# wo of one head as two 64-row halves on partitions 0 to 63, by two 32-row loads in eight shares

## The chip, the cores and the metric

The kernel runs on one core of a Trainium2 chip. The metric is the device time of one execution in microseconds. Before the change three runs took 711.59, 712.06 and 712.72 us; the median, 712.06 us, is what the change is compared with.

## The reference

Two layers, applied twice with the same weights, to a batch of four rows of 640 numbers (one token each, decoding from a cache). All is float32.

```python
x = x + _A_ref(_layernorm(x), k_cache, v_cache, wq, wo)   # round one
x = x + _B_ref(_layernorm(x), w1, w2)
x = x + _A_ref(_layernorm(x), k_cache, v_cache, wq, wo)   # round two
x = x + _B_ref(_layernorm(x), w1, w2)

# _A_ref: 32 heads of 128, the last W = 1024 positions of the cache
q = (x @ wq).reshape(B, 1, 32, 128).transpose(0, 2, 1, 3)
scores = einsum("bhqd,bhkd->bhqk", q, k[:, :, -W:]) * 128 ** -0.5
o = einsum("bhqk,bhkd->bhqd", softmax(scores), v[:, :, -W:])
return o.reshape(B, 1, 4096) @ wo                          # wo: 4096 x 640

# _B_ref: relu(x @ w1) @ w2, with w1 640 x 1728 and w2 1728 x 640
```

The head that the change touches is the 26th (number 25 counted from 0) in round one: its part of the last product is `o[:, 25] @ wo[25 * 128 : 26 * 128]`, 128 rows of 640.

## The kernel before

**Data.** The caches and weights of a head lie in HBM as one record of REC = 9472 columns on 128 partitions (the tensor `rec`): 640 columns of wq, 4096 of k, 4096 of v, 640 of wo, in this order (`WQ`, `K`, `V`, `WO` are the columns at which they begin). 32 records are 155 MB. They are read in round one and again in round two but for what is left in SBUF of the last heads. The tensor `wm` holds w1 and w2.

**Places in SBUF.** `store` has room for five records and a part of a sixth; `home(h, r)` says at which column a head's record goes. `kept` holds a part of head 26, `ring` (4320 columns) the MLP's weights in the time between the rounds; its first 128 columns hold an identity at the start, and until the MLP's first load nothing else is in it.

**Loads.** All large loads stand in one list, `items`, in a fixed order, and are issued by SyncE (SP). `pump()` issues from the head of the list for as long as the next load's place is free (`live` is the list of taken places); `done()` is called behind the matmuls that read a piece last, gives its columns back and calls `pump()`. So the order of loads is that of the list, and when one starts is decided by who reads the place last. Most loads are runs of several heads (`GROUPS`, 4 to 8 MB); towards a round's end they become smaller. Head 25 of round one is one load of 9472 columns. Each load takes one of eight semaphores in turn, so SP also waits for the load eight places earlier.

At the end of round one (`ending`) the wo of the last six heads (LATE) comes last, behind all k and v. Then come the MLP's weights into `ring` and the free half of a record.

**Compute.** For each head TensorE makes the query (`query`), the scores (`scores`), the products with v (`values`), the transposed output (`output_T`, a matmul that ScalarE copies from PSUM to `oTs`) and the product with wo (`project`: four matmuls of 160 columns, each with all 128 rows, added up in the PSUM tile `acc`). Heads overlap: while head n is at `values`, head n+1 is at `softmax`, head n+2 at `query`. VectorE and ScalarE do the softmax. `InOrder` keeps each engine's instructions in the written order; since it makes the calls, nearly all rows of the profile have its line, L102, and are told apart by their tiles.

Of the kernel before, what the change touches and what calls it, by code (L numbers as in the profile page):

```python
# [81 lines left out]
FIVE = [REC + 6272, 2 * REC - 3072, 2 * REC - 3200]  # L82
LAST_FIVE = [REC + 4736, 2 * REC - 4736, REC, REC]
THREE = [REC + HALF, REC + HALF]
GROUPS = [{h: FIVE for h in range(0, 25, 5)}, {6: THREE, 9: FIVE, 14: FIVE, 19: LAST_FIVE}]


# [19 lines left out]


@with_exitstack
def decode_kernel(ctx: ExitStack, tc: tile.TileContext, xf, rec, wm, out):  # L110
    nc = tc.nc
    pe, dve, act, pool, sp = (InOrder(tc, e) for e in (nc.tensor, nc.vector, nc.scalar, nc.gpsimd, nc.sync))
    sb = ctx.enter_context(tc.tile_pool(name="sb", bufs=1))
# [10 lines left out]
    hT = scratch.rearrange("p (m j) -> p m j", j=32)  # L124
    oTs = sb.tile([P, LATE, B], F32, name="oTs")
    qT = sb.tile([P, B], F32, name="qT")
    of_batch = sb.tile([P, B], F32, name="of_batch")
    of_block = sb.tile([P, 4], F32, name="of_block")
    rows = sb.tile([P, 2 * B], F32, name="rows")
# [58 lines left out]
    buffers = {"store": store, "ring": ring, "kept": kept}  # L188

    def load(src, lo, hi, buf, col, parts):  # L190
        items.append((src[:, lo:hi], buf, col, hi - lo, parts))

    def place(buf, col):
        return ("store", spare + FROM + col) if buf == "spare" else (buf, col)
# [10 lines left out]

    def piece(r, h, lo, hi, buf="store", col=None):
        run(r, h * REC + lo, h * REC + hi, buf, home(h, r) + lo if col is None else col)


    def group(r, h, sizes):  # L210
# [21 lines left out]
    for h in hs[:-3]:  # L232
        if h in GROUPS[0]:
            group(0, h, GROUPS[0][h])
        if h >= 25:
            piece(0, h, 0, KEPT if h == LAST - 1 else WO if h >= H - LATE else REC)
        if h == LAST - 1:
            piece(0, h, KEPT, WO, "kept", 0)
    ending(0, hs, True)
# [38 lines left out]
    def pump():  # L278

        while items:  # L280
            src, buf, col, n, parts = items[0]
            if any(b == buf and x < col + n and col < y for b, x, y in live):
                return
            sp.dma_start(buffers[buf][:, col:col + n], src)
            live.append((buf, col, col + n))
            for key, lo, hi, c in parts:
                at.setdefault(key, []).append((lo, hi, buf, c))
            items.pop(0)
# [1 line left out]
    def pieces(key):  # L290
        return at[key if key in at else (key[0], 0) + key[2:]]

    def cols(key, lo, n):

        for x, y, buf, col in pieces(key):
            if x <= lo and lo + n <= y:
                return buffers[buf][:, col + lo - x:col + lo - x + n]
        raise KeyError((key, lo, n))

    def done(key, lo, hi):  # L300
# [145 lines left out]
        dve.tensor_tensor(o, o, of_block.unsqueeze(2).to_broadcast([P, 4, DH]), op=OP.mult)  # L446
        dve.tensor_reduce(on[last], o.rearrange("p c d -> p d c"), op=OP.add, axis=AX.X)

    def output_T(i, last=False, to=None):
        to = outs[last][:, :B] if to is None else to  # L450
        pe.matmul(to, on[last], pick, start=True, stop=True)
        act.copy(oTs[:, i], to)

    def project(r, h, i, end):
        key = ("rec", r, h)
        for n in range(NB):
            pe.matmul(acc[32 * n:32 * n + B, :FD], oTs[:, i], cols(key, WO + n * FD, FD),
                      start=False, stop=end, skip_group_check=True)
        done(key, WO, REC)
# [41 lines left out]
    for r in range(2):  # L501
        hs = order[r]
        late = LATE if r == 0 else 2
        center(384 * r, 128)
        query(r, hs[0], 0, True)
        if r:
            busy(192, warm)
        scores(r, hs[0], 0, True)
        softmax(0, (r, hs[1], 1))
        if r:  # L510
            unpark(2)
            unpark(3)
        weights(0, ((0, 1), (1, 2)))
        for n, h in enumerate(hs[:-2]):
            i = n - (H - late)
            s = (n + 1) % 2
            scores(r, hs[n + 1], s)
            if r and not n:
                busy()
            softmax(s)  # L520
            end = n == H - 3
            values(r, h)
            if end:
                for _ in range(4):
# [8 lines left out]
            output_T(max(i, 0), to=None if r and not n else t_ps[:, :B])  # L533
# [70 lines left out]
```

## Time and profile before

| what | before |
|---|---|
| device time, median of 3 runs (lowest, highest) | 712.06 us (711.59, 712.72) |
| span of the profiled execution | 710.7 us |
| what lies around the span, by the lowest and the highest run | 0.9 to 2.0 us |
| moved by DMA | 301.97 MB, mean 425 GB/s |
| TensorE / VectorE / ScalarE busy | 71% / 45% / 14% |
| mean granted clock of TensorE | 0.824 |

The span goes from the first to the last instruction of one execution. The profiled execution's own device time is not listed beside the runs, so it is taken to lie among the three. Shares of busy time are averages over the whole span; the two rounds, the MLP between them and the one at the end have different limits and are read one by one in the prediction.

### The profile page before, as it was taken

What the parts mean: (1) busy time and instruction counts of PE and PEld (TensorE: products, weight loads), DVE (VectorE), ACT (ScalarE), POOL (GpSimd) and SP (SyncE); (2) the same over time, 40 slices, a digit from 0 to 9 for tenths busy, and PEclk for the clock granted to TensorE, in tenths of its full rate; (3) what the DMA queues carried; (4) which work ended last, traced back from release to release, by engine and by line L of the source; (5) the groups of instructions that cost most, each with busy time, mean ns of one, the idle gap of its engine ahead of it and who ended that gap; (6) DMA issues with size and microseconds to landing.
All of it is one profiled execution on the core that took longest, in us unless ns stands there. A gap on an engine that the chain in (4) does not pass through costs nothing.

```text
span 710.7 us, 8613 instructions
## 1 busy us (share of the span) xinstructions
PE 502.4 (71%) x3722; PEld 199.5 (28%) x3722; DVE 317.4 (45%) x645; ACT 99.6 (14%) x210; POOL 1.1 (0%) x9
## 2 busy tenths in 40 slices
PE   0675677576677686868788998756577685695985
PEld 0331322231332222333223333322222231332322
DVE  2252344253443353546541866625244253453661
ACT  0210111011010110111130421201010011011120
POOL 0000000000000000000000000000000000000000
PEclk9987787677676778788999999969687677788899
DMA  9999999999999999999999999999999999999996
GB/s 397 436 416 451 422 435 447 417 435 447 420 429 451 427 429 420 425 444 420 426 404 396 411 425 434 447 429 436 442 431 433 434 428 436 430 427 421 430 427 281
DMA packets 12741, 301.97 MB, mean 425 GB/s; under 512 B 1424, under 2 KB 1568, under 8 KB 4640
## 3 DMA queue, kind: packets, MB, share of 16 engines
q1 hardware_dynamic: 12672, 301.42, 98.9%
q8 instruction: 29, 0.48, 0.2%
q14 instruction: 8, 0.07, 0.0%
q10 hardware_dynamic: 32, 0.01, 0.0%
HBM read 301.34 MB, written 0.08 MB: 424 GB/s over the span
## 4 chain that ended last, share of the span: by engine, by line
DMA 68%; PE 25%; DVE 4%; another core or an unknown queue 1%; ACT 1%; issue 1%; SPq 0%; ACTq 0%
DMA store<-rec 60%; PE sc_ps L102 10%; PE o_ps L102 7%; DMA store<-wm 5%; PE acc L102 3%; PE misc L102 3%; DMA ring<-wm 3%; DVE scratch L102 2%; DVE o_ps L102 2%; PE t_ps L102 2%; ACT oTs L102 1%; DVE small L102 0%; ACT sc_ps L102 0%; DVE sc_ps L102 0%
## 5 line engine op out<-in xcount | busy, mean ns | idle before, releaser
L102 PE MATMUL sc_ps<-store,qT 128*4 128x512 f32 x1024 | 193.7, 852 | 37.8 <-DMA store<-rec 36.4
L102 PE MATMUL misc<-xT,store 128*128 128x4 f32 x620 | 92.8, 276 | 100.6 <-DMA store<-rec 100.0
L102 DVE TENSOR_REDUCE small<-sc_ps 128x1 f32<-128x1024 f32 x64 | 78.4, 1224 | 157.9 <-PE sc_ps L102 157.8
L102 PE MATMUL o_ps<-store,scratch 128*16 128x512 f32 x960 | 142.1, 667 | 4.6 <-DVE scratch L102 2.9
L102 PEld LDWEIGHTS misc<-xT,store 128*128 128x128 f32 x620 | 87.4, 221 | 156.2 <-DMA store<-rec 123.1
L102 ACT ACTIVATE sc_ps<-sc_ps,small 128x1024 f32<-128x1024 f32 x64 | 69.8, 1091 | 325.2 <-DVE small L102 325.2
L102 DVE STREAM_TRANSPOSE sc_ps<-sc_ps 128x1024 f32<-128x1024 f32 (+1 forms) x70 | 81.7, 1167 | 0.1
L102 PEld LDWEIGHTS sc_ps<-store,qT 128*4 128x4 f32 x1024 | 32.7, 107 | 121.2 <-issue 66.4
L102 PEld LDWEIGHTS o_ps<-store,scratch 128*16 128x16 f32 x960 | 32.3, 114 | 118.6 <-issue 100.7
L102 DVE TENSOR_TENSOR o_ps<-o_ps,of_block 128x512 f32<-128x512 f32 x62 | 43.4, 699 | 45.9 <-PE o_ps L102 45.8
L102 DVE TENSOR_TENSOR qT<-misc,rows 128x4 f32<-128x4 f32 x61 | 9.5, 156 | 112.7 <-PE misc L102 112.6
L102 PE MATMUL acc<-store,oTs 128*4 128x160 f32 x488 | 34.6, 365 | 17.1 <-ACT oTs L102 17.0
L102 DVE TENSOR_REDUCE scratch<-o_ps 128x128 f32<-128x512 f32 x62 | 42.9, 692 | 2.1
L102 ACT COPY oTs<-t_ps 128x4 f32<-128x4 f32 x59 | 9.6, 162 | 204.5 <-PE t_ps L102 204.5
L102 PE MATMUL t_ps<-rows,scratch 128*128 128x4 f32 x118 | 25.5, 286 | 11.4 <-DVE scratch L102 10.9
L102 PEld LDWEIGHTS t_ps<-rows,scratch 128*128 128x128 f32 x118 | 21.4, 226 | 17.9 <-DVE scratch L102 14.2
L102 DVE TENSOR_TENSOR scratch<-sc_ps,mrt 128x128 f32<-128x128 f32 (+1 forms) x70 | 19.6, 280 | 2.7
L102 PE MATMUL acc<-kept,small 128*1 128x328 f32 (+2 forms) x54 | 17.4, 428 | 0.0
L99 PE MATMUL acc<-scratch,ring 128*128 128x160 f32 x2 | 0.9, 540 | 22.2 <-DMA scratch<-xf 22.2
L102 DVE TENSOR_SCALAR mrt<-of_batch,small 128x4 f32<-128x4 f32 x64 | 14.7, 230 | 2.2
L102 DVE STREAM_TRANSPOSE scratch<-small 128x32 f32<-128x32 f32 x64 | 12.9, 202 | 2.4 <-ACT sc_ps L102 2.4
L102 PEld LDWEIGHTS acc<-store,oTs 128*4 128x4 f32 x488 | 6.9, 84 | 22.9 <-ACT oTs L102 21.9
(84 smaller groups left out, 123.1 us busy)
## 6 DMA issues: line engine op xcount, KB each, us to landing
store<-rec SPq DMA_DIRECT2D x14, 7872.0 KB, 28.9
store<-rec SPq DMA_DIRECT2D x7, 7936.0 KB, 30.9
store<-rec SPq DMA_DIRECT2D x4, 7104.0 KB
store<-rec SPq DMA_DIRECT2D x11, 2368.0 KB, 34.8
store<-rec SPq DMA_DIRECT2D x3, 4736.0 KB, 27.2
store<-rec SPq DMA_DIRECT2D x2, 4416.0 KB, 28.3
store<-rec SPq DMA_DIRECT2D x5, 1024.0 KB, 20.2
store<-rec SPq DMA_DIRECT2D x1, 4160.0 KB, 20.7
```

Source lines behind the costliest of these rows:

```text
L99: r = build(*args, **kwargs)
L102: r = build(*args, **kwargs)
```

## The change

The record of head 25 is loaded without its wo (8832 columns instead of 9472). Its wo comes from a new tensor in HBM, `halves`, by two more loads, into `ring` columns 128 to 1407: rows 0 to 63 of the wo stand in the first 640 of these columns, rows 64 to 127 in the other 640, both on partitions 0 to 63. Each of the two loads fills 32 partitions with rows of 1280 columns (5120 bytes). The source of a load is written as eight groups of four rows, with a fifth row between groups that is not read, so that its outermost dimension has eight steps.

The product with wo is then made in eight matmuls of 64 rows instead of four of 128. The second four need rows 64 to 127 of the transposed output on partitions 0 to 63; ScalarE makes this copy, `upper`, beside the usual one.

```diff
+SPLIT = 25
+HALVES_AT = 128
...
+    upper = sb.tile([64, B], F32, name="upper")
...
+    def halves_of(r):
+        shares = [(halves[q][:, :4], 32 * q, 32) for q in range(2)]
+        items.append((shares, "ring", HALVES_AT, 2 * D, [(("halves", r), 0, 2 * D, HALVES_AT)]))
...
-            piece(0, h, 0, KEPT if h == LAST - 1 else WO if h >= H - LATE else REC)
+            piece(0, h, 0, KEPT if h == LAST - 1 else WO if h >= H - LATE or h == SPLIT else REC)
+            if h == SPLIT:
+                halves_of(0)
...
-            sp.dma_start(buffers[buf][:, col:col + n], src)
+            for src, row, rows in shares:
+                sp.dma_start(buffers[buf][row:row + rows, col:col + n], src)
...
-    def output_T(i, last=False, to=None):
+    def output_T(i, last=False, to=None, split=False):
         pe.matmul(to, on[last], pick, start=True, stop=True)
         act.copy(oTs[:, i], to)
+        if split:
+            act.copy(upper, to[64:])
...
     def project(r, h, i, end):
         key = ("rec", r, h)
+        if (r, h) == (0, SPLIT):
+            key = ("halves", r)
+            for half, o in ((0, oTs[:64, i]), (1, upper)):
+                for n in range(NB):
+                    pe.matmul(acc[32 * n:32 * n + B, :FD], o, cols(key, half * D + n * FD, FD, 64), start=False,
+                              stop=False, skip_group_check=True)
+            done(key, 0, 2 * D)
+            return
...
+    halves = np.zeros((2, 8, 5, 2 * D), k.dtype)
+    halves[:, :, :4] = np.concatenate([rec[SPLIT, :64, WO:], rec[SPLIT, 64:, WO:]], 1).reshape(2, 8, 4, 2 * D)
```

On SP, the queue of loads near the end of round one's large groups; before, the row of 9472 columns is head 25, the two below it are head 26:

```order
L102 DMA store<-rec 128x15744
L102 DMA store<-rec 128x9472
L102 DMA store<-rec 128x6784
L102 DMA kept<-rec 128x2048
L102 DMA store<-rec 128x8832 x2
```

With the change, the same place:

```order
L104 DMA store<-rec 128x15744
L104 DMA store<-rec 128x8832
L104 DMA ring<-halves 32x1x1280 x2
L104 DMA store<-rec 128x6784
L104 DMA kept<-rec 128x2048
L104 DMA store<-rec 128x8832 x2
```

Head 25's load is shorter by 640 columns, and two loads of 32 rows stand between it and head 26; all later loads keep their order and stand two places further back.

On TensorE, the product with wo of head 25 (`acc`) before, behind the query of head 27 (`misc`) and ahead of that head's scores and of head 26's product with v (`o_ps`, half of it from `kept`):

```order
L102 MATMUL misc<-xT,store 128x4 x5
L102 MATMUL t_ps<-rows,scratch 128x4
L102 MATMUL acc<-store,oTs 4x160 x4
L102 MATMUL sc_ps_74<-store,qT 4x512 x8
L102 MATMUL o_ps<-store,scratch 16x512 x4
L102 MATMUL o_ps<-kept,scratch 16x512 x4
```

With the change:

```order
L104 MATMUL misc<-xT,store 128x4 x5
L104 MATMUL t_ps<-rows,scratch 128x4
L104 MATMUL acc<-ring,oTs 4x160 x4
L104 MATMUL acc<-ring,upper 4x160 x4
L104 MATMUL sc_ps_75<-store,qT 4x512 x8
L104 MATMUL o_ps<-store,scratch 16x512 x4
L104 MATMUL o_ps<-kept,scratch 16x512 x4
```

Four matmuls on `oTs` and `store` have become eight, four on `oTs` and four on `upper`, all reading `ring`; nothing else on TensorE has moved. The new tile `upper` takes 32 bytes of each partition ahead of `store`, `kept` and `ring`, which all begin 32 bytes further on.

More of the change, by code (lines that the diff above doesn't have):

```diff
@@ L109, in decode_kernel @@
 @with_exitstack
-def decode_kernel(ctx: ExitStack, tc: tile.TileContext, xf, rec, wm, out):
+def decode_kernel(ctx: ExitStack, tc: tile.TileContext, xf, rec, halves, wm, out):
     nc = tc.nc
@@ L190, in load @@
     def load(src, lo, hi, buf, col, parts):
-        items.append((src[:, lo:hi], buf, col, hi - lo, parts))
+        items.append(([(src[:, lo:hi], 0, P)], buf, col, hi - lo, parts))
     def place(buf, col):
@@ L280, in pump @@
         while items:
-            src, buf, col, n, parts = items[0]
+            shares, buf, col, n, parts = items[0]
             if any(b == buf and x < col + n and col < y for b, x, y in live):
                 return
-            sp.dma_start(buffers[buf][:, col:col + n], src)
+            for src, row, rows in shares:
+                sp.dma_start(buffers[buf][row:row + rows, col:col + n], src)
             live.append((buf, col, col + n))
@@ L291, in pieces, with cols @@
         return at[key if key in at else (key[0], 0) + key[2:]]
-    def cols(key, lo, n):
+    def cols(key, lo, n, rows=P):
         for x, y, buf, col in pieces(key):
             if x <= lo and lo + n <= y:
-                return buffers[buf][:, col + lo - x:col + lo - x + n]
+                return buffers[buf][:rows, col + lo - x:col + lo - x + n]
         raise KeyError((key, lo, n))
@@ L532, in decode_kernel @@
                 busy(320, sc_ps[n % 2])
-            output_T(max(i, 0), to=None if r and not n else t_ps[:, :B])
+            output_T(max(i, 0), to=None if r and not n else t_ps[:, :B], split=(r, h) == (0, SPLIT))
             if r and not n:
@@ L592 @@
         "rec": rec.transpose(1, 0, 2).reshape(P, H * REC),
+        "halves": halves,
         "wm": np.concatenate([block_rows(np.asarray(B_w1)).transpose(1, 0, 2).reshape(P, KB * FF), *tiles], 1),
```

## The prediction, made before the change was run

> **What bounds the kernel.** I read the page first, then the chain of waits, then the busy time by windows.
>
> ```profile
> span 710.7 us, 8613 instructions
> PE 502.4 (71%) x3722; PEld 199.5 (28%) x3722; DVE 317.4 (45%) x645; ACT 99.6 (14%) x210; POOL 1.1 (0%) x9
> DMA  9999999999999999999999999999999999999996
> q1 hardware_dynamic: 12672, 301.42, 98.9%
> q8 instruction: 29, 0.48, 0.2%
> q14 instruction: 8, 0.07, 0.0%
> q10 hardware_dynamic: 32, 0.01, 0.0%
> DMA 68%; PE 25%; DVE 4%; another core or an unknown queue 1%; ACT 1%; issue 1%; SPq 0%; ACTq 0%
> ```
>
> The 16 DMA engines are busy in every slice; the loads' queue q1 alone fills 98.9% of 16 engines' span. No compute engine comes near. So the time is that of moving 301 MB, and what can still differ is how evenly the 16 engines are loaded and whether any of them runs out of work. The windows show both (columns: the window, its length, busy time of PE, PEld, DVE, ACT and POOL, granted clock, DMA share, GB/s):
>
> ```profile
> 300.00:357.00 57.00, 43.78 (x322) 16.95 (x322) 31.41 (x60) 8.90 (x20) 0.00 (x0) 0.88 1.00 429
> 357.00:372.00 15.00, 12.56 (x112) 3.77 (x112) 6.63 (x20) 5.14 (x10) 0.00 (x0) 1.00 1.02 406
> 372.00:400.00 28.00, 23.41 (x239) 9.76 (x240) 11.11 (x30) 5.20 (x9) 0.00 (x0) 1.00 1.00 394
> 400.00:702.00 302.00, 224.19 (x1684) 88.35 (x1685) 147.29 (x294) 43.36 (x95) 0.00 (x0) 0.82 1.00 432
> 702.50:703.00 0.50, 0.48 (x12) 0.10 (x2) 0.00 (x0) 0.00 (x0) 0.00 (x0) 1.00 0.91 379
> 703.00:703.50 0.50, 0.00 (x0) 0.00 (x0) 0.00 (x0) 0.00 (x0) 0.00 (x0) 1.00 0.74 307
> 703.50:704.00 0.50, 0.00 (x0) 0.00 (x0) 0.00 (x0) 0.00 (x0) 0.00 (x0) 1.00 0.64 261
> 704.00:704.50 0.50, 0.00 (x0) 0.00 (x0) 0.00 (x0) 0.00 (x0) 0.00 (x0) 1.00 0.54 220
> 704.50:705.00 0.50, 0.13 (x4) 0.11 (x8) 0.00 (x0) 0.00 (x0) 0.00 (x0) 1.00 0.39 159
> 705.00:705.50 0.50, 0.50 (x20) 0.40 (x16) 0.00 (x0) 0.00 (x0) 0.00 (x0) 1.00 0.42 169
> 705.50:706.00 0.50, 0.50 (x24) 0.39 (x20) 0.00 (x0) 0.00 (x0) 0.00 (x0) 1.00 0.42 140
> 706.00:706.50 0.50, 0.50 (x19) 0.35 (x14) 0.00 (x0) 0.00 (x0) 0.00 (x0) 1.00 0.17 67
> 706.50:707.00 0.50, 0.50 (x20) 0.34 (x10) 0.00 (x0) 0.00 (x0) 0.00 (x0) 1.00 0.04 15
> ```
>
> The last nine rows are the uneven end. The DMA share falls from 0.91 to 0.04 over some 4.5 us: the engines finish the same list of loads one after another, half of them by about 704.3 (0.54 of 16), one alone after 706.5, until about 706.8 (0.04 x 16 x 0.5 us is 0.3 us). The shares add up to 4.27, times 0.5 us 2.1 us: had all 16 ended together, it would have been at about 704.6, some 2.2 us sooner. That is the most that any evening out can bring.
>
> The unevenness has a cause in the first list: q8, 29 instruction packets in 0.48 MB, 16 KB each. Its 0.2% of 16 engines' span (0.15 to 0.25) is 17 to 28 us, 0.6 to 1.0 us a packet, and the engine that serves one falls behind the others by that and a little more. Followed from packet to packet in the trace's records (each engine's next packet starts where its last one ended), every fetch sets one engine back by about 1.4 us, and the fetches go round eight engines in a fixed order, three or four each; the other eight serve none, only some of the eight small q14 packets. So the eight engines that end last are, all but one, those with fetches. The 32 packets of q10 (the four loads of x, four rows each, with their semaphores) fall on the same four engines each time, none of them in the fetches' rotation, though one of the four runs level with another for a while and is placed by its trend alone.
>
> **The moved bytes.** 432 GB/s over 16 engines is 27.0 GB/s for one. Before, an engine carries 8 of the 128 rows of each load: 8 x 2560 bytes of this wo, 20,480 bytes or 0.76 us. All 16 engines lose that. The two new loads have eight shares of four rows of 5120 bytes each: 40,960 bytes or 1.52 us on each of eight engines, and with ten small packets' overhead (a 4-byte packet of q1 lasts 9 ns in the records) some 1.55 us or a little more. So eight engines carry 0.76 us less and eight 0.79 us more. Which eight is what counts. A load in few shares took the same engines four times over (q10), so I expect eight shares on a fixed set that contains these four. If it is the set without fetches, the engine that ends last, at 706.8, ends 0.76 us sooner, at 706.0. Of the loaded ones most end by 704.3 and the latest, as the records go, at 705.2; with 0.79 us more that is 706.0 too, level with the relieved ones. I take **0.7 us less**; the bounds are 0.76 less and 0.79 more.
>
> [...]
>
> [...]
>
> ```profile
> SPq L102 <- PE acc L102: 355.7, 33, 27.0
> SPq L102 <- DMA store<-rec: 114.2, 18, 38.7
> store<-rec SPq DMA_DIRECT2D x14, 7872.0 KB, 28.9
> store<-rec SPq DMA_DIRECT2D x11, 2368.0 KB, 34.8
> ```
>
> SP waits for places (PE acc) and for the load eight places earlier (DMA store<-rec); still a load lands 29 to 35 us after its issue (last number of the last two rows). At the new loads' place the engines thus have some 30 us of work queued, and the eight that carry none go straight on to head 26. Two more issues and a shift of two in the turn of the eight semaphores cost nothing under that cover; if it were gone, they would cost two issues, below 1 us.
>
> **TensorE and ScalarE at head 25.**
>
> ```profile
> 320.40 0.16 ACT L102 COPY oTs<-t_ps 128x4 f32<-128x4 f32 x1 [7.40 <-PE t_ps L102]
> 320.62 0.71 PE L102 MATMUL acc<-store,oTs 128*4 128x160 f32 x8 [0.31 <-ACT oTs L102]
> 321.11 3.38 PE L102 MATMUL sc_ps<-store,qT 128*4 128x512 f32 x16
> 325.42 2.88 SPq L102 DMA_DIRECT2D store<-rec  x3
> 328.00 1.28 PE L102 MATMUL misc<-xT,store 128*128 128x4 f32 x10 [1.79 <-DMA store<-rec]
> ```
>
> The product with wo starts 0.49 us ahead of the scores (320.62 to 321.11), so doubling it adds 0.5 us, at most the 0.71 us of the row; 64 rows instead of 128 may cost less, and I have no row of that, so nothing to 0.71. The copy to `upper` is another 0.16 us and lies beside the first four matmuls. Behind them on TensorE stand head 27's scores and head 26's product with v, and for the latter waits SP with the loads at 325.42: these start up to 0.9 us later, under 30 us of queued work. TensorE itself waits 1.79 us for a load at 328.00, which takes up the rest. Cost: nothing; uncovered, 0.5 to 0.9 us. The MLP's first load into `ring` now also waits for this product, which is over 35 us sooner.
>
> **Between the rounds**, 357 to 400, the rate falls to 406 and 394 GB/s: the mean engine idles 15 x (1 - 406/432) + 28 x (1 - 394/432) = 3.4 us. There a relieved engine's gain could be lost.
>
> ```profile
> 369.66 6.76 DMA ring<-wm
> 378.88 6.69 DMA ring<-wm
> 385.61 1.30 PE acc L102 x30
> ```
>
> These pieces of the chain of waits are loads on whose last engine the MLP waits and whose end lets the next be issued. The whole stage follows the slowest engine; the early ones idle for it. In the records the slowest finds its next load always queued, with 1.4 us or more to spare, so its gain is kept. Of the loaded eight, one is already 3.1 us behind the first here (after a q14 packet), and 0.79 us more makes it last by some 0.2 us: issues come that little later, within the spare time.
>
> **The sum.** Against the profiled execution: span 710.7 - 0.7 = 710.0 us. The same 0.7 us off the median gives 712.06 - 0.7 = 711.4 us.
>
> **Rivals.**
> - *The gain is lost between the rounds.* If the fetching engines do run dry there, the 0.76 us of round one is idled away and the second half begins as before: 712.1 us. For it speak the 394 GB/s, against it the spare time.
> - *The loaded eight include the last one.* Then it carries 0.79 us more: 712.06 + 0.79 = 712.85 us, slower. It decides as soon as one engine with four fetches is among them; only four of the eight are placed by the records.
> - *The shares are not eight.* Spread over all 16, the bytes are as before: 712.1 us.
> - *The new place costs.* All of `store` moves by 32 bytes. If each packet took one 32-byte step more (32 / 27.0 = 1.2 ns), the 12672 / 16 = 792 packets of an engine would cost 0.94 us: 711.4 + 0.9 = 712.3; from two steps on, 713.2 and more, it is slower than a measurement's doubt. No row shows such a cost, none excludes it.
>
> **How the numbers follow.** The forecast gets 0.56, the lost gain 0.16, the loaded last engine 0.12, no eight shares 0.05, the cost of the place 0.06; 0.05 remain for a gain over 1.4 us, where an earlier MLP helps more than counted. 0.2% (1.4 us) is about what a measurement of this kernel can tell from no change, and the three runs before lie 1.1 us apart. The first four cases all lie within it. Their spread by half a microsecond to either side and the last two give faster 0.10, within 0.82, slower 0.08. The range goes from 710.5, the forecast with such a spread and a little, to 712.9, the loaded last engine: below and above it lie about 0.08 and 0.1.
>
> **What will show it.** Right: in windows of 0.5 us at the end the DMA share falls more steeply and reaches 0 about 0.7 us sooner in the span; the two new loads land some 30 us after issue; the product with wo of head 25 shows 16 rows on TensorE and a wait for a load still stands ahead of head 28's query. Wrong: the share's tail as long as before or longer (the wrong engines), a lower rate from 357 to 400 (gain lost), or below 432 GB/s from 400 to 702 (the place costs).

## The result and the profile after

| | before | after |
|---|---|---|
| device time, median (lowest to highest) | 712.42 us (711.59 to 712.72, 5 runs) | 716.4 us (716.07 to 716.79, 5 runs) |
| ratio after to before, 95% interval | | 1.0056 [1.0044, 1.0068] |
| span of the profiled execution | 710.7 us | 714.4 us |

The change makes the kernel about 4 us (0.6%) slower; the forecast was 711.4 us, and the range ended at 712.9. The same lines of the page as before, now with the change (its line L102 is L104 here):

```profile
span 714.4 us, 8633 instructions
PE 502.9 (70%) x3730; PEld 201.7 (28%) x3730; DVE 317.4 (44%) x645; ACT 99.7 (14%) x211; POOL 1.1 (0%) x9
DMA  9999999999999999999999999999999999999996
q1 hardware_dynamic: 12752, 301.42, 98.9%
q8 instruction: 29, 0.48, 0.3%
DMA 67%; PE 24%; DVE 4%; another core or an unknown queue 3%; ACT 1%; issue 1%; SPq 0%; ACTq 0%
```

Nothing has changed in what bounds it. The loads move the same 301.42 MB, in 80 packets more, the queue still fills 98.9% of 16 engines' span, and that span is 3.7 us longer. So the same bytes took longer on engines that were as busy as before. The windows (columns as in the prediction, the last one GB/s) say where. The first row is of before, the others are with the change:

```profile
0.00:300.00 300.00, 194.77 (x1282) 78.45 (x1282) 120.60 (x242) 36.96 (x77) 1.12 (x9) 0.79 1.00 430
0.00:300.00 300.00, 190.47 (x1280) 76.31 (x1280) 120.04 (x240) 36.96 (x77) 1.12 (x9) 0.80 1.00 429
300.00:357.00 57.00, 45.76 (x332) 17.64 (x331) 31.53 (x63) 8.52 (x20) 0.00 (x0) 0.85 1.00 425
357.00:372.00 15.00, 11.26 (x107) 3.43 (x109) 7.19 (x20) 5.68 (x10) 0.00 (x0) 1.00 1.00 395
372.00:400.00 28.00, 22.77 (x231) 8.74 (x231) 9.08 (x28) 3.99 (x7) 0.00 (x0) 1.00 0.99 381
400.00:702.00 302.00, 226.69 (x1672) 92.40 (x1665) 147.85 (x291) 44.58 (x97) 0.00 (x0) 0.79 1.00 430
705.50:706.00 0.50, 0.50 (x22) 0.40 (x16) 0.00 (x0) 0.00 (x0) 0.00 (x0) 1.00 0.91 374
707.00:707.50 0.50, 0.00 (x0) 0.00 (x0) 0.00 (x0) 0.00 (x0) 0.00 (x0) 1.00 0.58 236
709.00:709.50 0.50, 0.50 (x22) 0.39 (x17) 0.00 (x0) 0.00 (x0) 0.00 (x0) 1.00 0.34 133
710.00:710.50 0.50, 0.50 (x20) 0.39 (x16) 0.00 (x0) 0.00 (x0) 0.00 (x0) 1.00 0.05 20
```

From 400 to 702 us, far behind the change and with a DMA share of 1.00 both times, the rate is 430 GB/s and was 432: 0.5% less, on loads that the change does not touch. Between the rounds it falls more (395 and 381 against 406 and 394). At the end the share falls from 0.91 to 0.05 between 705.5 and 710.5 us; before it did so between 702.5 and 707.

A rate that is lower everywhere points at the single packet. The trace's records hold each packet's duration. Here are the medians of three sizes (62,976 bytes are 15,744 columns of one partition), and the time of all q1 packets, summed up and divided by 16 engines:

| kernel | 62,976 B | 18,944 B | 6912 B | all q1 packets / 16 |
|---|---|---|---|---|
| before | 2324 ns | 705 ns | 262 ns | 703.15 us |
| after | 2327 ns | 708 ns | 266 ns | 706.31 us |

Three to four nanoseconds on the median packet of these sizes, and 4.5 on the mean one of all, are 3.16 us for an engine that serves 708 of them one behind the other (12,752 less 1424 of 4 bytes, which still take 9 ns, by 16). The slowdown also begins ahead of the new loads. Load by load, the landing on the first engine to finish is 0.06 to 0.15 us later than before in the first five loads, up to 96 us, and 0.63 us at 282 us, where the new loads are still to come. The moved bytes take 0.7 off behind that. Then it is 0.84 at 369 us, 2.5 at 388 and 3.57 at the last load: some 1.7 us of it arise in 20 us between the rounds, the rest a little at a time.

### The profile page after: what moved, and what is told of

Read it like the earlier page. It is cut to its first block, busy times and chain, and to the rows that moved or that the text cites. A ratio compares the mean times of both kernels' runs of the same rounds, so it can differ in the third digit from the quotient of the medians.

```text
span 714.4 us, 8633 instructions
## 1 busy us (share of the span) xinstructions
PE 502.9 (70%) x3730; PEld 201.7 (28%) x3730; DVE 317.4 (44%) x645; ACT 99.7 (14%) x211; POOL 1.1 (0%) x9
## 3 DMA queue, kind: packets, MB, share of 16 engines
q1 hardware_dynamic: 12752, 301.42, 98.9%
## 4 chain that ended last, share of the span: by engine, by line
DMA 67%; PE 24%; DVE 4%; another core or an unknown queue 3%; ACT 1%; issue 1%; SPq 0%; ACTq 0%
DMA store<-rec 59%; PE sc_ps L104 9%; PE o_ps L104 7%; DMA store<-wm 5%; PE misc L104 3%; DMA ring<-wm 3%; PE acc L104 3%; DVE scratch L104 2%; PE t_ps L104 2%; DVE o_ps L104 1%; ACT oTs L104 1%; DVE small L104 0%; ACT sc_ps L104 0%; DVE sc_ps L104 0%
## 5 line engine op out<-in xcount | busy, mean ns | idle before, releaser
L104 PE MATMUL sc_ps<-store,qT 128*4 128x512 f32 x1024 | 188.9, 831 | 40.8 <-DMA store<-rec 39.4
L104 PE MATMUL misc<-xT,store 128*128 128x4 f32 x620 | 95.2, 280 | 100.0 <-DMA store<-rec 99.3
L104 DVE TENSOR_REDUCE small<-sc_ps 128x1 f32<-128x1024 f32 x64 | 78.4, 1224 | 156.6 <-PE sc_ps L104 156.4
L104 PE MATMUL o_ps<-store,scratch 128*16 128x512 f32 x960 | 144.2, 677 | 4.3 <-DVE scratch L104 3.0
L104 PEld LDWEIGHTS misc<-xT,store 128*128 128x128 f32 x620 | 89.8, 226 | 157.0 <-DMA store<-rec 122.3
L104 ACT ACTIVATE sc_ps<-sc_ps,small 128x1024 f32<-128x1024 f32 x64 | 69.8, 1091 | 323.4 <-DVE small L104 323.4
L104 DVE STREAM_TRANSPOSE sc_ps<-sc_ps 128x1024 f32<-128x1024 f32 (+1 forms) x70 | 81.7, 1167 | 0.1
L104 PEld LDWEIGHTS sc_ps<-store,qT 128*4 128x4 f32 x1024 | 31.9, 104 | 122.1 <-issue 64.9
L104 PEld LDWEIGHTS o_ps<-store,scratch 128*16 128x16 f32 x960 | 32.2, 113 | 115.8 <-issue 99.3
L104 DVE TENSOR_TENSOR o_ps<-o_ps,of_block 128x512 f32<-128x512 f32 x62 | 43.4, 699 | 48.1 <-PE o_ps L104 48.0
L104 DVE TENSOR_TENSOR qT<-misc,rows 128x4 f32<-128x4 f32 x61 | 9.5, 156 | 114.6 <-PE misc L104 114.6
L104 PE MATMUL acc<-store,oTs 128*4 128x160 f32 x480 | 33.1, 356 | 18.2 <-ACT oTs L104 16.7
L104 DVE TENSOR_REDUCE scratch<-o_ps 128x128 f32<-128x512 f32 x62 | 42.9, 691 | 2.1
L104 ACT COPY oTs<-t_ps 128x4 f32<-128x4 f32 x59 | 9.6, 162 | 208.8 <-PE t_ps L104 208.8
L104 PE MATMUL t_ps<-rows,scratch 128*128 128x4 f32 x118 | 25.5, 287 | 11.8 <-DVE scratch L104 11.1
L104 PEld LDWEIGHTS t_ps<-rows,scratch 128*128 128x128 f32 x118 | 21.5, 227 | 18.1 <-DVE scratch L104 14.8
L104 DVE TENSOR_TENSOR scratch<-sc_ps,mrt 128x128 f32<-128x128 f32 (+1 forms) x70 | 19.6, 280 | 2.7
L104 PE MATMUL acc<-kept,small 128*1 128x328 f32 (+2 forms) x54 | 17.4, 428 | 0.0
L104 DVE TENSOR_SCALAR mrt<-of_batch,small 128x4 f32<-128x4 f32 x64 | 14.7, 229 | 2.2
L104 DVE STREAM_TRANSPOSE scratch<-small 128x32 f32<-128x32 f32 x64 | 12.9, 202 | 2.4 <-ACT sc_ps L104 2.4
L104 PEld LDWEIGHTS acc<-store,oTs 128*4 128x4 f32 x480 | 6.7, 84 | 24.1 <-ACT oTs L104 21.5
## 6 DMA issues: line engine op xcount, KB each, us to landing
store<-rec SPq DMA_DIRECT2D x14, 7872.0 KB, 29.5
```

The costliest lines, as they stand in the source:

```text
L104: r = build(*args, **kwargs)
```

## The experiments

The change does two things that could lengthen packets or unbalance engines: `upper` is allocated ahead of `store`, `kept` and `ring` and shifts them by 32 bytes (`store` begins at byte 3104 of each partition instead of 3072, which is 12 x 256), and eight engines carry the moved wo. The first four kernels take these apart. Each kernel's ratio is to runs of the kernel before on the same chip, whose medians were 712.6, 712.55, 712.3 and 711.81 us in the four groups of runs.

### The place of `store`

`upper_behind` is the change with `upper` behind `ring`, so that `store` is back at 3072:

```diff
-    upper = sb.tile([64, B], F32, name="upper")
     of_batch = sb.tile([P, B], F32, name="of_batch")
...
     ring = sb.tile([P, RING], F32, name="ring")
+    upper = sb.tile([64, B], F32, name="upper")
```

> The changed kernel, but with the 32-byte tile upper behind ring in SBUF, so that store, kept and ring begin where they did before the change (store at byte 3072, a multiple of 256). The loads in eight shares and the eight matmuls stay. Theory 1, the place of store costs (each packet of the loads lasts some 3 to 6 ns longer when its target is 32 bytes off): the time falls from 716.4 back to 711.5 to 712.8 us, and the loads' largest packets last as long as before. Theory 2, the loads in eight shares cost (their eight engines finish later and the MLP between the rounds waits for them): it stays at 715.5 to 716.5 us. Theory 3, TensorE's and ScalarE's extra work at head 25 costs: it stays there too.

`gap32` and `gap64` are the kernel before with an unused tile of 32 or 64 bytes at the place where `upper` stands in the change:

```diff
     qT = sb.tile([P, B], F32, name="qT")
+    gap = sb.tile([P, 8], F32, name="gap")     # 16 columns in gap64
```

> The kernel before, with nothing but an unused tile of 32 bytes ahead of store, so that store, kept and ring begin at 32 modulo 256 as in the changed kernel. Theory 1 (the place costs): 715.2 to 716.8 us, that is all or nearly all of the change's loss without any of its loads and matmuls. Theories 2 and 3: 712.4 us, as before.

> The kernel before with an unused tile of 64 bytes ahead of store: store, kept and ring at 64 modulo 256. Theory 1 in two forms. If any start off a multiple of 256 bytes costs the same: 715 to 717 us. If what counts is a multiple of 64: 712.4 us. Theories 2 and 3: 712.4 us.

`at128` is the kernel before with two tiles of 128 bytes together behind `ring`, so that `store` begins at 2944, 128 above a multiple of 256:

```diff
-    oTs = sb.tile([P, LATE, B], F32, name="oTs")
-    qT = sb.tile([P, B], F32, name="qT")
...
     ring = sb.tile([P, RING], F32, name="ring")
+    oTs = sb.tile([P, LATE, B], F32, name="oTs")
+    qT = sb.tile([P, B], F32, name="qT")
```

> The kernel before with the small tiles oTs and qT behind ring instead of ahead of store: store, kept and ring at 128 modulo 256. Theory 1: if any start off a multiple of 256 costs, 715 to 717 us; if 64 or 128 are enough, 712.4 us. Theories 2 and 3: 712.4 us. (What moves oTs and qT to another address could cost by itself; nothing in the trace of before makes that likely.)

Later `at2816` did the same with the six tiles from `oTs` to `mrt`, 256 bytes together, in the same lines: 2816 is 11 x 256 and no multiple of 512.

> The kernel before with six small tiles (oTs, qT, of_batch, of_block, rows, mrt: 256 bytes) allocated behind ring, so that store begins at byte 2816 = 11 x 256 instead of 3072 = 12 x 256. Theory 256: packets are lengthened only where they start off a multiple of 256 bytes; then the time is that of before, about 712.5 us, ratio 1.000, and the median packet of 62,976 bytes lasts 2324 ns. Theory 512 (or 1024): 3072 is a multiple of both, 2816 of neither; then it is as with 128 bytes, about 714.9 us, ratio 1.0036, packet 2326 ns. If the small tiles' own place matters (they are read and written by all engines), it is neither.

The columns on packets are as in the table above, in ns.

| kernel | `store` modulo 256 | median | ratio to before | 62,976 B | 18,944 B | 6912 B | all q1 / 16 |
|---|---|---|---|---|---|---|---|
| upper_behind | 0 | 713.24 us | 1.0012 [1.0003, 1.0021] | 2324 | 705 | 262 | 703.19 us |
| gap32 | 32 | 715.73 us | 1.0046 [1.0031, 1.0061] | 2327 | 708 | 266 | 705.51 us |
| gap64 | 64 | 715.12 us | 1.0040 [1.0025, 1.0055] | 2326 | 707 | 265 | 705.20 us |
| at128 | 128 | 714.88 us | 1.0036 [1.0023, 1.0050] | 2326 | 706 | 264 | 705.10 us |
| at2816 | 0 | 712.24 us | 0.9993 [0.9982, 1.0003] | 2324 | 705 | 262 | 703.30 us |

Of the theories the first, the place, holds for the bulk, and the other two do not. `gap32`, in which nothing of the change is left but 32 unused bytes, is slower by most of what the change is. (`upper_behind` comes out a little above the 712.8 us that the theory allowed it.) Its windows (from the profiled execution, 717.51 us, its slowest) show the rate of the kernel after:

```profile
0.00:300.00 300.00, 188.13 (x1282) 77.11 (x1282) 120.93 (x244) 36.99 (x77) 1.13 (x9) 0.81 1.00 429
300.00:357.00 57.00, 41.45 (x317) 16.68 (x320) 30.88 (x59) 8.52 (x20) 0.00 (x0) 0.88 1.00 425
400.00:702.00 302.00, 221.07 (x1668) 88.00 (x1667) 147.99 (x294) 44.59 (x97) 0.00 (x0) 0.82 1.00 430
```

In `at2816`, where the same tiles lie elsewhere but `store` begins on a multiple of 256 again, it is that of the kernel before:

```profile
0.00:300.00 300.00, 189.53 (x1280) 76.39 (x1280) 120.38 (x242) 36.99 (x77) 1.13 (x9) 0.80 1.00 430
300.00:357.00 57.00, 44.51 (x322) 17.32 (x322) 31.50 (x62) 8.83 (x20) 0.00 (x0) 0.85 1.00 428
400.00:702.00 302.00, 224.10 (x1664) 91.89 (x1668) 147.18 (x293) 43.73 (x97) 0.00 (x0) 0.81 1.00 432
```

So the median packet lasts 1 to 4 ns longer in the kernels whose targets begin 32, 64 or 128 bytes off a multiple of 256, and as long as before (2324, 705 and 262 ns) in `at2816`; this excludes that it must be a multiple of 512. How far off makes little difference (2.0 to 2.4 us of packets for 128, 64 and 32 bytes, the nearest start costing most). That part of the change costs 0.4 to 0.5%, and `upper_behind` still is slower than before by 0.1%, where the forecast had a gain of 0.1%. The other experiments are about this remainder.

The lengthening is not there all the time, though the targets are off all the time. In `gap32`, `gap64`, `at128` and the change, the first four loads, up to some 77 us, have the medians of before (2324 ns for 62,976 bytes, 2342 for 63,488); from the seventh load on, at 114 us, they are 2325 to 2328 and 2345 to 2347. The seventh load has the same size and goes to the same place as the fourth. From 375 to 395 us, between the rounds, the median of every load is again that of before (385 ns for 10,240 bytes, for example). So it is not a fixed price of each packet with such a target. What else has to come together for it, no run shows.

### The eight shares

A share is the part of a load that one engine carries. In the records of before, the packets of the first 366 us (some 5100) fall into 16 sequences, one for each engine, with eight rows of every load in the order of issue, and all but about one in a hundred packets of the whole trace start within 60 ns of where another ends. So a trace can be followed engine by engine; which engines carry the new loads is seen directly, because only eight of the 16 sequences have packets of 5120 bytes at that place (in the change, 64 of them, eight on each). In `upper_behind` at some 357 us, as round one's last loads land:

| engines | instruction fetches served so far | behind the first engine |
|---|---|---|
| first (no load of halves) | none | 0 |
| latest of the eight without halves | two | 3.5 us |
| latest of the eight with halves | two | 4.4 us |

Two of the eight engines in the fetches' rotation are among the loaded ones, in this trace and in that of the change. An even load was to show whether that is the loss. `sixteen` writes each source in sixteen groups of two rows, and `four` goes the other way, with four groups of eight (the lines that fill the groups go with them):

```diff
-        shares = [(halves[q][:, :4], 32 * q, 32) for q in range(2)]
+        shares = [(halves[q][:, :2], 32 * q, 32) for q in range(2)]     # sixteen
+        shares = [(halves[q][:, :8], 32 * q, 32) for q in range(2)]     # four
...
-    halves = np.zeros((2, 8, 5, 2 * D), k.dtype)
+    halves = np.zeros((2, 16, 3, 2 * D), k.dtype)                       # sixteen
+    halves = np.zeros((2, 4, 9, 2 * D), k.dtype)                        # four
```

> As upper_behind (store at its old place, the wo in two 32-row loads into ring, eight matmuls and the second copy), but the source of each of the two loads is written in sixteen groups of two rows instead of eight of four, so that each of the 16 engines carries 20,480 bytes, as before the change. Question: where do the 0.6 to 0.9 us come from that upper_behind is still slower than before (713.24 against 712.6, ratio 1.0012)? Theory A, the balance: eight engines carry 0.79 us more, and two of these eight also serve instruction fetches; the engine that ends last is one of them. Then sixteen shares take the loss away: about 712.5 us, ratio 1.000. Theory B, the split: the eight matmuls, the copy, the two more loads or their place in ring cost it, whichever engines carry the bytes. Then about 713.2 us, ratio 1.0012.

> As upper_behind, but each source in four groups of eight rows: four engines carry 81,920 bytes (some 3.05 us, 2.3 us more than before the change), twelve carry 0.76 us less. In the traces the four engines of a load in four shares serve no instruction fetches. Theory A (what counts is whether a loaded engine also serves fetches): none of the four is among the last, the fetching engines are relieved by 0.76 us; between the rounds and at the end the four become level with the last or a little later: 711.9 to 712.7 us, ratio 0.999 to 1.000, less than upper_behind. Theory A' (a load in few shares costs by how long its few engines take, whichever they are): 1.5 us more than upper_behind, about 714.7 us, ratio 1.003. Theory B (split): as upper_behind, about 713.2 us, ratio 1.0012.

And `eight_double` puts a double amount on the same eight engines (rows of `4 * D` columns, of which the second half is not read):

```diff
-        items.append((shares, "ring", HALVES_AT, 2 * D, [(("halves", r), 0, 2 * D, HALVES_AT)]))
+        items.append((shares, "ring", HALVES_AT, 4 * D, [(("halves", r), 0, 4 * D, HALVES_AT)]))
...
-    halves = np.zeros((2, 8, 5, 2 * D), k.dtype)
+    halves = np.zeros((2, 8, 5, 4 * D), k.dtype)
```

> As upper_behind, but each row of the two loads in eight shares is 10,240 bytes instead of 5120, the second half of which nothing reads: 320 KB more, all on the same eight engines. The loaded eight carry 0.79 + 1.52 = 2.3 us more than before the change, the mean engine 0.76 us more. Theory A (the balance: the last engine is a loaded one): the time follows the loaded engines, about 712.5 + 2.3 = 714.8 us, ratio 1.0032. Theory B (the split; the engines even out): upper_behind and the mean's 0.76 us, about 714.0 us, ratio 1.002.

Neither `sixteen` (715.04 us, ratio 1.0033 [1.0021, 1.0045]) nor `four` (716.72 us, 1.0055 [1.0043, 1.0067]) came out as any of the theories had it, and `eight_double` (713.97 us, 1.0019 [1.0010, 1.0028]) lay nearer to theory B. The reason for the first two stands in a window of 6 us at the new loads. First the kernel before and, below it, `upper_behind`, both as even as the stages around:

```profile
292.00:298.00 6.00, 5.67 (x42) 1.58 (x42) 3.23 (x7) 0.60 (x2) 0.00 (x0) 0.72 0.94 402
292.00:298.00 6.00, 6.00 (x45) 1.77 (x45) 2.94 (x4) 0.89 (x1) 0.00 (x0) 0.72 1.00 424
```

then `sixteen`:

```profile
292.00:298.00 6.00, 5.69 (x42) 1.43 (x42) 3.08 (x5) 0.58 (x2) 0.00 (x0) 0.72 0.95 287
```

and `four`:

```profile
292.00:298.00 6.00, 6.00 (x47) 1.81 (x35) 2.93 (x4) 1.21 (x2) 0.00 (x0) 0.72 1.03 308
```

A quarter of the rate or more is gone while the engines are busy all the time; this is called the dip below. In the records the packets of the neighbouring loads last up to 1.9 us instead of 1006 ns (27,136 bytes), and those of the new loads up to 450 ns instead of 196. Three kernels were made to find out why. `from_rec` reads no new tensor:

```diff
-        shares = [(halves[q][:, :4], 32 * q, 32) for q in range(2)]
-        items.append((shares, "ring", HALVES_AT, 2 * D, [(("halves", r), 0, 2 * D, HALVES_AT)]))
+        for q in range(2):
+            src, col = rec[64 * q:64 * q + 64, SPLIT * REC + WO:(SPLIT + 1) * REC], HALVES_AT + q * D
+            items.append(([(src, 0, 64)], "ring", col, D, [(("halves", r), q * D, q * D + D, col)]))
```

> As upper_behind (store at its old place, eight matmuls of 64 rows, the second copy, the wo in ring on partitions 0 to 63), but the two halves come from rec itself, by two loads of 64 rows of 2560 bytes, so that each of the 16 engines carries 8 x 2560 = 20,480 bytes as before the change and no new tensor is read. It leaves nothing of the change but the split compute and the two more loads. Theory A (upper_behind's loss is the uneven load): as before, 712.3 to 712.6 us, ratio 1.000, and the last engine of the loads behind the halves lands within 0.3 us of where it lands in the kernel before (in upper_behind 0.5 us later, in eight_double 1.8 us). Theory B (the split costs): as upper_behind, about 713.2 us, ratio 1.0012, with the MLP or the end later although the loads behind the halves land as before. Theory C (a load into 64 partitions is slow in itself): these loads land later, as in the kernel sixteen (2.2 us).

`sixteen_behind_wm` is `sixteen` with the tensor `halves` declared behind `wm`:

```diff
-def decode_kernel(ctx: ExitStack, tc: tile.TileContext, xf, rec, halves, wm, out):
+def decode_kernel(ctx: ExitStack, tc: tile.TileContext, xf, rec, wm, halves, out):
```

> The kernel sixteen, with the tensor halves declared behind wm instead of ahead of it, which alters where halves and wm lie in HBM and nothing else. In sixteen's trace all packets that are read beside those of halves last longer (27,136 bytes 1006 ns before, up to 1.8 us there) for some 6 us from 292 us on, and every load behind lands 2.1 us later on all engines; upper_behind and eight_double read a tensor halves as well and show nothing of it. Theory P (it is where the rows of halves lie in HBM as against the rows of rec): another place takes it away, and the time is that of from_rec, 712.4 to 713.2 us, ratio at most 1.0012. Theory F (it is the form: sixteen shares of two rows, 15,360 bytes apart): the packets are as long as in sixteen and the time is about 715.0 us, ratio 1.0033.

`eight_crossed` keeps eight shares and their bytes and alters only which rows a share has:

```diff
-        shares = [(halves[q][:, :4], 32 * q, 32) for q in range(2)]
+        shares = [(halves[:, :8], 0, 64)]
...
-    halves = np.zeros((2, 8, 5, 2 * D), k.dtype)
+    halves = np.zeros((8, 9, 2 * D), k.dtype)
```

> As upper_behind, but the 64 rows come in one load, in eight shares of eight neighbouring rows (0 to 7, 8 to 15 and so on) instead of two loads in eight shares of four: the same packets of 5120 bytes and the same 40,960 bytes on each of the eight engines, but each engine now writes other partitions. In upper_behind share s writes rows 4s to 4s + 3 and 32 + 4s to 35 + 4s. In sixteen, four, from_rec and sixteen_behind_wm, where the shares were cut in other ways, all packets read at that time lasted up to 1.8 times as long and the loads behind landed 2 to 4 us later. Theory P (what matters is that each engine keeps to a fixed set of partitions, rows 4s and 32 + 4s; two engines that write into the same set hold each other up): packets last longer here too, the loads behind land some 2 us later and the time is about 715 us, ratio 1.0035. Theory N (eight shares are good, four and sixteen are not): as upper_behind, ratio 1.001, packets of 5120 bytes 196 ns.

All three show the dip. `from_rec`, `sixteen_behind_wm` and `eight_crossed`, in this order:

```profile
292.00:298.00 6.00, 5.39 (x39) 1.60 (x43) 3.61 (x8) 0.74 (x2) 0.00 (x0) 0.72 0.96 262
```

```profile
292.00:298.00 6.00, 5.49 (x42) 1.57 (x42) 3.42 (x8) 0.64 (x2) 0.00 (x0) 0.72 0.95 257
```

```profile
292.00:298.00 6.00, 4.68 (x46) 1.62 (x45) 4.53 (x10) 1.37 (x3) 0.00 (x0) 1.00 1.00 290
```

| kernel | median | ratio to before | last landing of the 27,136-byte load behind the halves, against before |
|---|---|---|---|
| from_rec | 714.44 us | 1.0032 [1.0021, 1.0042] | +2.75 us |
| sixteen_behind_wm | 714.72 us | 1.0029 [1.0018, 1.0041] | +2.98 us |
| eight_crossed | 715.9 us | 1.0060 [1.0044, 1.0076] | +2.08 us |

So it is neither the place in HBM (theory P of `sixteen_behind_wm` falls) nor the number of shares (theory N of `eight_crossed` falls). `eight_crossed` differs from `upper_behind` in nothing but the rows that a share has (and in one load instead of two), and has the dip (290 GB/s instead of 424): its theory P holds in that, for which `from_rec` and its theory C had been a first sign. That two engines hold each other up, as theory P has it, was not shown. Its time is longer than theory P had it (ratio 1.0060, 1.0035 expected), and the dip's own 2.08 us do not account for that: the last landing is 2.7 us late ahead of the MLP and 3.8 behind it. The two 32-row loads in eight shares of four rows are the one form of those tried that writes 64 partitions without it.

With the even load out of reach, the remainder was settled from the other two sides: the compute alone, and a third dose. `upper_behind_again` repeats the first dose:

> The kernel upper_behind once more, beside from_rec and on the same chip, since the difference in question (0.6 to 0.9 us) is little more than an interval. Theory A: again 713.0 to 713.4 us, ratio 1.001, some 0.7 us above from_rec. Theory B: the same time as from_rec.

`split_alone` has the loads of the kernel before and only the split compute:

```diff
     def project(r, h, i, end):
         key = ("rec", r, h)
+        if (r, h) == (0, SPLIT):
+            for o in (oTs[:64, i], upper):
+                for n in range(NB):
+                    pe.matmul(acc[32 * n:32 * n + B, :FD], o, cols(key, WO + n * FD, FD, 64), start=False,
+                              stop=False, skip_group_check=True)
+            done(key, WO, REC)
+            return
```

> The kernel before (all loads as there, store at its place) with the change's compute alone: head 25's product in eight matmuls of 64 rows and ScalarE's second copy, to upper behind ring. Both times four matmuls take rows 0 to 63 of the wo, the second four with the copy of the output's rows 64 to 127, so rows 64 to 127 of this wo are left out. Theory B (what upper_behind is still slower, 0.4 to 0.7 us or ratio 1.0008 to 1.0012, is the split compute): ratio 1.001, 713.0 us. Theory A (it is the uneven load): ratio 1.000, 712.3 us, and all loads land as before.

`eight_triple` is `eight_double` with rows of `6 * D` columns:

```diff
-        items.append((shares, "ring", HALVES_AT, 4 * D, [(("halves", r), 0, 4 * D, HALVES_AT)]))
+        items.append((shares, "ring", HALVES_AT, 6 * D, [(("halves", r), 0, 6 * D, HALVES_AT)]))
```

> As upper_behind, but the rows of the two loads in eight shares are 15,360 bytes, two thirds of which nothing reads: 640 KB more on the same eight engines. These carry 0.79 + 3.05 = 3.8 us more than before the change, the mean engine 1.5 us more. Theory A (the time follows the loaded engines): 1.52 us more for each 320 KB, 712.4 + 3.8 = 716.2 us, ratio 1.0053. Theory M (the time follows the mean engine, since what the loaded ones are late is taken up behind): 0.76 us for each 320 KB: 712.9 + 1.5 = 714.4 us, ratio 1.0029. eight_double (ratio 1.0019 against 1.0008 and 1.0012) stood between the two, nearer to M.

| kernel | dose on the eight, against before | median | ratio to before | span | last landing of the load behind |
|---|---|---|---|---|---|
| split_alone | none | 712.25 us | 1.0001 [0.9992, 1.0009] | 710.0 us | +0.23 us |
| upper_behind | +0.79 us | 713.24 us | 1.0012 [1.0003, 1.0021] | 711.5 us | +0.49 us |
| upper_behind_again | +0.79 us | 712.68 us | 1.0008 [1.0000, 1.0017] | 710.9 us | -0.23 us |
| eight_double | +2.3 us | 713.97 us | 1.0019 [1.0010, 1.0028] | 712.5 us | +1.85 us |
| eight_triple | +3.8 us | 715.79 us | 1.0056 [1.0042, 1.0070] | 714.1 us | +3.49 us |

The split compute shows no cost: the interval of `split_alone` ends at 1.0009, just below theory B's 1.001. The third dose gives what theory A had, 1.0053, and not theory M's 1.0029. The second dose taken by itself would have misled: its median lies nearer to the other theory, though its loads land 1.85 us later as theory A has it. In `upper_behind_again` the load behind the halves ends sooner than before, but at the MLP's first load the last engine is 0.43 us late, as in `upper_behind` (0.41). Ahead of the MLP in `eight_triple` the latest loaded engine is 7.2 us behind the first and the latest of the others 3.3 us. Its windows between the rounds show what waits for that engine:

```profile
357.00:372.00 15.00, 12.42 (x114) 3.62 (x106) 8.48 (x21) 5.84 (x11) 0.00 (x0) 0.96 0.98 386
372.00:400.00 28.00, 22.81 (x232) 9.01 (x236) 7.97 (x26) 4.00 (x7) 0.00 (x0) 1.00 0.99 380
```

against 409 and 397 GB/s in `split_alone`:

```profile
357.00:372.00 15.00, 12.38 (x112) 3.58 (x104) 6.50 (x18) 4.52 (x9) 0.00 (x0) 1.00 1.03 409
372.00:400.00 28.00, 23.54 (x240) 9.76 (x240) 11.26 (x32) 5.20 (x9) 0.00 (x0) 1.00 1.00 397
```

The MLP's loads into `ring` follow one another through places that come free when the last engine has landed, so the engines that were relieved idle there: the first engine's landing, 0.3 us sooner than before ahead of the MLP, is 3.2 us later at 423 us, where the last engine's is 3.1 us later.

## Why the prediction was wrong, point by point

- **What bounds the kernel**: right. The DMA engines are full in both, and every result above is read from packets and landings.
- **The new place costs** (a rival at 0.06) is what happened, and its price is the step that failed. The prediction took "one 32-byte step more (32 / 27.0 = 1.2 ns)" a packet, 0.94 us, which was its author's estimate, said of two steps and more that it "is slower than a measurement's doubt", and gave little chance to either. (Of the 792 packets that it counted, 88 are the 4-byte ones.) Measured: 3 to 4 ns on the median packet for most of the time, 2.36 us of packets in `gap32`, whose ratio is 1.0046, and 3.16 us in the change as a whole. No row of before could give the price, but the prediction let the missing row count as a reason for a small chance; as an unknown on all packets of an engine it belonged into the range. The runs agree with a multiple of 256 (`at2816` as before, `at128` slower). They do not agree with a price that grows with the distance from the multiple below (with 32 bytes the packet of 62,976 takes 3 ns longer, with 128 only 2), nor with one that every such packet pays (none in the first four loads).
- **"If it is the set without fetches"**: this step of the moved bytes failed too. Two of the eight loaded engines serve fetches, so the rival "the loaded eight include the last one" occurred, at 712.85 us; `upper_behind`, which is the change without its shift, measures 713.24 and 712.68 us. The sizes were about right: in `upper_behind` the first engine's landings behind the halves come 0.5 to 0.6 us sooner (0.76 expected), and the remainder of 0.6 to 0.9 us (0.0008 to 0.0012 of 712.5) fits the 0.79 of the loaded ones.
- **The 30 us of queued work** were read wrongly. That the eight engines without halves "go straight on to head 26" is so (0.5 to 0.6 us sooner in `upper_behind`), but none of the queued work moved to them: in the records every load of 128 rows has eight on each engine, and the time followed the last engine's sum (3.8 us more on the loaded ones in `eight_triple`, ratio 1.0056). Sixteen shares were not the way out either: with the dip they came out slower still (`sixteen`, 1.0033).
- **Queue and semaphores**: right. The two new loads are issued at 265.5 and 266.4 us and end at 296.5 and 297.3, some 31 us behind the issue; the median of the large loads is 29.5:

```profile
265.54 1.57 SPq L104 DMA_DIRECT2D ring<-halves  x2
store<-rec SPq DMA_DIRECT2D x14, 7872.0 KB, 29.5
```

- **TensorE and ScalarE at head 25**: right, and now with rows. In the kernel after, the product begins 1.17 us ahead of the scores instead of 0.49, 0.68 more where the prediction had at most 0.71. Of the 1.79 us that TensorE waited ahead of head 28's query some 0.1 are left there (328.75 to 328.87), so the cover was just enough. The split is only a part of that: the granted clock from 325 to 329 us was 0.66 there and 1.00 before, and `o_ps` from `kept` begins 2.50 us later than before, of which 0.80 stand already at `acc` and 0.68 are the split:

```profile
321.20 0.16 ACT L104 COPY oTs<-t_ps 128x4 f32<-128x4 f32 x1 [7.52 <-PE t_ps L104]
321.39 0.16 ACT L104 COPY upper<-t_ps 64x4 f32<-64x4 f32 x1
321.42 0.71 PE L104 MATMUL acc<-ring,oTs 64*4 64x160 f32 x8 [0.31 <-ACT oTs L104]
321.91 0.75 PE L104 MATMUL acc<-ring,upper 64*4 64x160 f32 x8
322.59 3.59 PE L104 MATMUL sc_ps<-store,qT 128*4 128x512 f32 x16
327.67 1.08 PE L104 MATMUL o_ps<-kept,scratch 128*16 128x512 f32 x8
328.87 1.28 PE L104 MATMUL misc<-xT,store 128*128 128x4 f32 x10
```

  In `split_alone`, where nothing else differs, 1.16 us of the wait are left, and its ratio of 1.0001 shows the cover by itself:

```profile
328.58 1.28 PE L104 MATMUL misc<-xT,store 128*128 128x4 f32 x10 [1.16 <-DMA store<-rec]
```

- **Between the rounds**: that 0.79 us more would make one of the loaded engines last "by some 0.2 us" was right; in the change, at 358 us, the last engine is a loaded one, 4.0 us behind the first, and the next is 3.8 us behind. But "so its gain is kept" needed a slowest engine that was relieved; there was none, and the rival of the lost gain came true as well. In `upper_behind` the MLP's first loads land 0.4 us later than before on their last engine and 0.56 us sooner on their first; at 423 us the first engine is 0.29 us later than before, so the lead of the relieved engines is gone.

```profile
357.00:372.00 15.00, 11.71 (x108) 3.43 (x102) 5.83 (x15) 3.70 (x7) 0.00 (x0) 1.00 1.01 409
372.00:400.00 28.00, 23.08 (x239) 9.73 (x240) 10.87 (x30) 5.04 (x9) 0.00 (x0) 1.00 0.99 388
```

  These two rows, of `upper_behind`, are 406 and 394 before. By the prediction's formula the mean engine idles 3.7 us in them (15 x (1 - 409/432) + 28 x (1 - 388/432)), where it was 3.4.
- **The sum.** Two rivals came true together: 1.0046 (`gap32`) times 1.0008 to 1.0012 (the two runs of `upper_behind`) is 1.0054 to 1.0058, and the change measures 1.0056. The range was built from one rival at a time, and ended at the larger of those it believed.

What stays open: why the start costs 3 ns rather than 1, why it costs nothing in the first four loads and from 375 to 395 us, and whether the second dose's small ratio is chance (its interval reaches 1.0028, theory A had 1.0032) or because the fetches of its second half fell on other engines. None of the kernels tried is clearly faster than the one before; the change does best as `upper_behind`, and that is still 0.1% slower.

## What to carry to other kernels

In a kernel that is bound by its transfers, keep the first byte of every large DMA target on a multiple of 256, and look at the addresses after adding even a tile of 16 bytes a partition (it takes up 32): allocated ahead of the big buffers it costs 0.4 to 0.5% here, behind them nothing that could be measured. Moving bytes between DMA engines brought nothing here, since the engine that ended last was not relieved (`upper_behind`, 1.0012 and 1.0008), so follow the engines through the trace first, with all that they also serve, and know which of them the new load's shares fall on. Where an unknown price multiplies by hundreds of packets, give it room in the range, and let two rivals add up.

## What the runs showed of the hardware

- **A target's start 32, 64 or 128 bytes off a multiple of 256** went with a median packet 1 to 4 ns longer, at 6912 bytes as much as at 62,976 (264 to 266 ns instead of 262, 2326 to 2327 instead of 2324), but not in the first 77 us and not from 375 to 395 us. Here that is 2.0 to 2.4 us of an engine's 703 us of packets (`at128`, `gap64`, `gap32`).
- **Which rows a share has** mattered to the neighbouring loads. In the three kernels with eight shares of rows 4s to 4s + 3 and 32 + 4s to 35 + 4s (`upper_behind`, `eight_double`, `eight_triple`) the packets of the new loads (5120, 10,240 and 15,360 bytes) take 196, 385 and 573 ns throughout. With rows 8s to 8s + 7 (`eight_crossed`), or with 4 or 16 shares, the same rows cost the whole core a quarter of its rate or more for some 6 us (257 to 308 GB/s instead of 402 to 424). The neighbouring loads' packets of 27,136 bytes last up to 1.9 us in `sixteen` and `four` instead of 1006 ns. What causes it was not shown.
- **Matmuls of 64 rows** lasted as long as those of 128 at 160 columns: the first four take 0.71 us in the row above, as the four of 128 rows did before the change, both at a granted clock of 0.50 (320 to 322 us).
